# Attention on one core: the V product of a unit is copied out of PSUM in two halves, by ScalarE and by VectorE

## The chip, the cores and the metric

The kernel runs on one core of a Trainium2 chip. The core has a matrix engine (TensorE, PE in the profile, its weight loads PEld), three engines for elementwise work (VectorE or DVE, ScalarE or ACT, GpSimd or POOL) and SyncE (SP), which here only issues DMA transfers. Each engine works through its own queue in order, and they wait for each other by semaphores. TensorE writes its products to PSUM, eight banks of 128 partitions by 512 fp32 columns; the other engines bring them from there to SBUF. The metric is the device time of one execution in microseconds. A change of the kernel counts as a change of time from 0.2% on.

## The reference

One transformer block on 2048 tokens of width 512, with adaptive layer norms. Attention has 32 heads of width 16, softmax over all 2048 keys, and a feed-forward part of width 1792 follows.

```
h = layernorm(x) * (1 + ca) + sa                  # sa, ca, ga, ... = silu(c) @ w_mod
q, k, v = split_heads(h @ wqkv)                   # 32 heads of 16
p = softmax(q @ k.T / 4)
x = x + ga * ((p @ v) merged @ wo)
h = layernorm(x) * (1 + cb) + sb
x = x + gb * (gelu(h @ w1 + b1) @ w2 + b2)
```

## The kernel before

The program has three stages. In the first, up to about 304 us, it normalizes the tokens, transposes them and computes Q, K and V; it also begins with the row maxima of the scores. The second is attention, up to about 1411 us. The third is the output projection and the feed-forward part.

**Units and steps.** Attention runs over 32 units. A unit u is a group of 4 heads and a block of 512 queries (`g, qb = divmod(u, NB)`). A unit has 16 steps of 128 keys, numbered through as s (`NS = NU * NKC` of them). In a step TensorE makes four score blocks of 128 keys by 512 queries, one for each head (`exp_step`, L860, tokens X0 to X3, tile sc), ScalarE takes the exponential of each (L861, tile p), and TensorE multiplies the four blocks of the step before with V (`pv_step`, L693, token P). The four heads of a V product go to four column groups of the array, so that one PSUM tile pv holds 32 rows for each head: 16 rows of the product, then the row of the denominators. The sum over the unit's 16 steps is formed in that tile.

**Row maxima.** The exponentials of a unit need its row maxima. They are made ahead: a step also has three maxima blocks (tokens M0 and M1, `max_bank`): a matmul into a tile mx (L429) and a row maximum of its 512 columns on VectorE (L431). When a unit's 64 are done, a small reduction (L465), two GpSimd instructions and a transpose (L475) bring them into the form in which they are stored and loaded as additional rows of Q. For the first nine units this happens in the first stage, so the maxima run out some 20 steps before the end of attention.

**Order.** The order within a step is written out by hand and alternates between two lists; the V product P of step s - 1 stands in step s:

```
ORDER = ("X0 X1 M1 X2 M0 X3 P M1".split(), "X0 X1 X2 M0 M0 X3 P M1".split())
```

After a step's tokens come the other tasks that are due there: `todo` (among them the transpose of L475) and `hooks` (among them the split of the output weights, with a cast on VectorE, L709, at steps 24, 32, 40 and 48). PSUM in this stage has 3 banks for mx, 4 for sc and 1 for pv. So the last V product of a unit, the copy of its tile and the first V product of the next unit follow one another on one bank.

**The copy.** When the last step's V product has been issued, in step s = 16(u + 1), `attn_out` copies pv into the SBUF tile osb (128 by 512, two buffers) by one ScalarE activation (L680) and issues five stores: the products of the four heads (L682) and the denominators (L683). They are read again, as o and den, only when the output projection of that query block is near.

Of the kernel before, what the change touches and what calls it, by code (L numbers as in the profile page):

```python
# [10 lines left out]
AF = mybir.ActivationFunctionType  # L11
# [14 lines left out]
TB = S // NB  # L26
# [26 lines left out]
def block_kernel(ctx: ExitStack, tc: tile.TileContext, x, wqkv, wo, w1, b1, w2, b2, c, w_mod, out):  # L53
    nc = tc.nc
    te, ve, ac, gp, sy = nc.tensor, nc.vector, nc.scalar, nc.gpsimd, nc.sync
# [621 lines left out]
    def attn_out(u, pv):  # L677
        g, qb = divmod(u, NB)
        o = ppool.tile([P, TB], F32, tag="osb", name="osb")
        ac.activation(o, pv, AF.Copy)  # L680
        for j in range(4):
            sy.dma_start(o_d[qb][g * 64 + j * DH : g * 64 + (j + 1) * DH], o[32 * j : 32 * j + DH])  # L682
        sy.dma_start(den_d[qb][g * 4 : (g + 1) * 4], o[DH::32])  # L683
# [3 lines left out]
    def pv_step(s):  # L687
        u, kc = divmod(s, NKC)
        g = u // NB
        if kc == 0:  # L690
            cur_pv[0] = bank_pv()
        for j in range(4):
            te.matmul(cur_pv[0][32 * j : 32 * (j + 1)], vg[g][:, kc, j * VW : j * VW + 32],  # L693
                      pt.pop((s, j)), start=kc == 0, stop=kc == NKC - 1)
        if kc == NKC - 1:
            attn_out(u, cur_pv[0])
# [329 lines left out]
```

## Time and profile before

| | |
|---|---|
| time, median of 3 runs (lowest to highest) | 1770.09 us (1769.41 to 1771.3) |
| the profiled execution | 1768.67 us |
| its span, from the first to the last instruction | 1766.9 us |
| mean granted TensorE clock | 0.995 |
| ScalarE, exponentials of L861 | 2048 instructions, 1055.3 us busy, mean 615 ns |
| VectorE, row maxima of L431 | 1472 instructions, 927.9 us busy, mean 684 ns |
| ScalarE, the copies of L680 | 32 instructions, 20.3 us busy, mean 633 ns |

A row of a timeline has the start in us from the start of the span, the length in us, the engine, the line of the kernel, the operation, output and input tile, shapes and the number of instructions merged in it; in square brackets the idle time of that engine before it and what ended that. A row of a group or of one line has the number of instructions and the least, median and largest duration in ns. A busy time can hold instructions that overlap in their engine's pipeline: the next one may start before the end of the last.

### The profile page before, as it was taken

How to read it: one execution, taken by the hardware profiler on the slowest of the kernel's cores; microseconds unless marked ns; L12 is line 12 of the kernel's file. 1: busy time of each engine (PE TensorE's matmuls, PEld its weight loads, DVE VectorE, ACT ScalarE, POOL GpSimd, SP SyncE). 2: the span in 40 equal slices, each digit the busy share in tenths (PEclk: the TensorE clock that was granted, in tenths of full speed). 3: DMA queues.
4: the chain of work that ended last, by engine and by line, in shares of the span. 5: the costliest groups of instructions: out<-in, count | busy, mean ns of one | idle time of the engine just before them, and what ended most of it. 6: DMA issues, size and time to landing. Idle time of an engine off the chain costs nothing.

```text
span 1766.9 us, 29171 instructions
## 1 busy us (share of the span) xinstructions
PE 1750.8 (99%) x10554; PEld 902.6 (51%) x10554; DVE 1405.3 (80%) x2553; ACT 1356.4 (77%) x2580; POOL 320.1 (18%) x347
## 2 busy tenths in 40 slices
PE   8999999999999999999999999999999999999998
PEld 6755555343343343343343334334333478788887
DVE  6579998898888888888888888888886286838453
ACT  3478887999999999999999999999999722213222
POOL 3204422011000000000000000000003154636462
PEclk9999999999999999999999999999999999999999
DMA  8767636811500410410411101101013064323341
GB/s 278 252 137 163 150 115 132 128 36 29 86 23 23 77 32 23 74 35 23 74 30 28 39 23 35 38 23 35 23 58 106 21 195 131 126 78 113 103 120 48
DMA packets 124100, 144.17 MB, mean 82 GB/s; under 512 B 38930, under 2 KB 72722, under 8 KB 122004
## 3 DMA queue, kind: packets, MB, share of 16 engines
q1 hardware_dynamic: 120644, 135.55, 30.6%
q10 hardware_dynamic: 3312, 6.76, 1.0%
q8 instruction: 83, 1.36, 0.3%
q14 instruction: 61, 0.50, 0.1%
HBM read 106.37 MB, written 35.87 MB: 81 GB/s over the span
## 4 chain that ended last, share of the span: by engine, by line
PE 93%; DVE 3%; issue 1%; DMA 1%; POOL 1%; SPq 0%; ACT 0%; ACTq 0%; DVEq 0%; POOLq 0%
PE pv L693 29%; PE mx L429 19%; PE sc L300 16%; PE sc L860 13%; PE mx L447 6%; PE mx L924 5%; PE pv L924 2%; PE sc L800 1%; PE mx L800 1%; DVE glo L907 0%; POOL w2l L731 0%; PE sc L257 0%; DMA rb<-rden 0%; PE mx L257 0%; DVE xin L278 0%
## 5 line engine op out<-in xcount | busy, mean ns | idle before, releaser
L861 ACT ACTIVATE p<-sc 128x512 f32<-128x512 f32 x2048 | 1055.3, 615 | 42.3 <-PE sc L860 16.8
L431 DVE TENSOR_REDUCE mxs<-mx 128x1 f32<-128x512 f32 x1472 | 927.9, 684 | 116.0 <-PE sc L860 78.6
L693 PE MATMUL pv<-p,vg 128*32 128x512 f32 x4096 | 546.8, 605 | 0.0
L860 PE MATMUL sc<-qst,kq 50*128 50x512 f32 x1024 | 284.7, 437 | 1.6 <-DVE mxf L458 1.6
L860 PE MATMUL sc<-qst,kt 50*128 50x512 f32 x1024 | 282.3, 431 | 0.0
L429 PE MATMUL mx<-kq,qmx 48*128 48x512 f32 x768 | 262.2, 428 | 0.2
L429 PE MATMUL mx<-kt,qmx 48*128 48x512 f32 x704 | 241.5, 430 | 0.0
L429 PEld LDWEIGHTS mx<-kq,qmx 48*128 48x128 f32 x768 | 122.6, 184 | 228.4 <-DVE mxs L431 209.3
L429 PEld LDWEIGHTS mx<-kt,qmx 48*128 48x128 f32 x704 | 114.0, 186 | 209.1 <-DVE mxs L431 191.5
L903 ACT ACTIVATE g<-sc,b_c 128x512 f32<-128x512 f32 x56 | 38.6, 690 | 237.2 <-PE sc L300 237.2
L458 DVE CUSTOM_DVE_ANT_0 cp<-mx,cp 128x512 f32<-128x512 f32 x288 | 186.9, 688 | 36.3 <-PE mx L447 31.4
L471 POOL CAST m<-mn 128x16 fp32r<-128x16 f32 x32 | 6.3, 197 | 1029.4 <-DVE mn L465 1029.4
L454 ACT ACTIVATE cp<-mx 128x512 f32<-128x512 f32 x288 | 156.4, 597 | 38.4 <-PE mx L447 38.1
L693 PEld LDWEIGHTS pv<-p,vg 128*32 128x32 f32 x4096 | 81.1, 108 | 181.2 <-issue 169.8
L860 PEld LDWEIGHTS sc<-qst,kq 50*128 50x128 f32 x1024 | 126.4, 186 | 33.7 <-ACT p L861 23.4
L907 DVE TENSOR_TENSOR glo<-g,ghi 128x512 fp32r<-128x512 f32 x56 | 60.2, 1075 | 94.7 <-ACT ghi L906 94.7
L860 PEld LDWEIGHTS sc<-qst,kt 50*128 50x128 f32 x1024 | 125.6, 185 | 10.1 <-ACT p L861 3.1
L447 PE MATMUL mx<-kt,qmx 48*128 48x512 f32 x576 | 113.0, 455 | 0.0
L729 POOL TENSOR_TENSOR w1l<-w1r,w1h 128x512 fp32r<-128x512 f32 x56 | 76.9, 1372 | 152.7 <-DVE w1h L728 130.5
L447 PEld LDWEIGHTS mx<-kt,qmx 48*128 48x128 f32 x576 | 58.3, 184 | 56.0 <-issue 33.8
L300 PE MATMUL sc<-hThi,w 128*128 128x512 f32 x256 | 84.1, 436 | 2.2 <-DVE hThi L263 2.2
L731 POOL TENSOR_TENSOR w2l<-w2r,w2h 128x512 fp32r<-128x512 f32 x56 | 81.1, 1448 | 6.6 <-DVE w2h L730 6.1
(158 smaller groups left out, 1672.8 us busy)
## 6 DMA issues: line engine op xcount, KB each, us to landing
w1r<-in_B_w_dram SPq DMA_DIRECT2D x56, 256.0 KB
w2r<-in_B_w_dram SPq DMA_DIRECT2D x56, 256.0 KB
qk<-parts SPq DMA_DIRECT2D x25, 512.0 KB
qmx<-qk SPq DMA_DIRECT2D x192, 64.0 KB
qst<-qk SPq DMA_DIRECT2D x192, 64.0 KB
wmod<-in_w_mod_dram SPq DMA_DIRECT2D x6, 1024.0 KB
kq<-qk SPq DMA_DIRECT2D x24, 256.0 KB
kt<-qk SPq DMA_DIRECT2D x24, 256.0 KB
```

Source lines behind the costliest of these rows:

```text
L300: te.matmul(ps, p, q, start=i == 0, stop=i == len(terms) - 1)
L429: te.matmul(ps, qmx[u][rows, p, qc * P : (qc + 1) * P], kst[u // NB][rows, p, kr * TB : (kr + 1) * TB], start=True, stop=True)
L431: ve.tensor_reduce(mxs[u][:, p, a, qc, kr : kr + 1], ps, axis=AX.X, op=ALU.max, negate=True)
L447: te.matmul(ps, qmx[u][rows, p, qc * P : (qc + 1) * P], kpm[u // NB][rows, p, t0 : t0 + TB], start=True, stop=True)
L454: ac.activation(vabs[n, a], ps, AF.Abs)
L458: ve.tensor_tensor_reduce(v, ps, v, -0.5, 3.0e38, ALU.add, ALU.min, mxs[u][:, p, a, qc, r : r + 1])
L693: te.matmul(cur_pv[0][32 * j : 32 * (j + 1)], vg[g][:, kc, j * VW : j * VW + 32], pt.pop((s, j)), start=kc == 0, stop=kc == NKC - 1)
L729: gp.tensor_tensor(alo, a, ahi.bitcast(F32), op=ALU.subtract)
L731: gp.tensor_tensor(blo, b, bhi.bitcast(F32), op=ALU.subtract)
L860: te.matmul(ps, k[r0 : r0 + KX, p, kc * P : (kc + 1) * P], q[r0 : r0 + KX, p], start=True, stop=True)
L861: ac.activation(pb, ps, AF.Exp, scale=SCALE)
L924: te.matmul(acc[qb][t], p[:, sl], q, start=f == 0 and n == 0, stop=f == NF - 1 and n == 2)
```

## The change

The one copy of 128 partitions by 512 columns becomes two of 256 columns. The first half of the queries is copied by ScalarE as before, the second half by VectorE with a plain copy. Source, destination, the five stores and the order of everything else stay the same; in VectorE's queue the new instruction stands where `attn_out` is called. In the changed kernel the lines behind it have numbers larger by 2.

```diff
     def attn_out(u, pv):
         g, qb = divmod(u, NB)
         o = ppool.tile([P, TB], F32, tag="osb", name="osb")
-        ac.activation(o, pv, AF.Copy)
+        h = TB // 2
+        ac.activation(o[:, :h], pv[:, :h], AF.Copy)
+        ve.tensor_copy(o[:, h:], pv[:, h:])
         for j in range(4):
             sy.dma_start(o_d[qb][g * 64 + j * DH : g * 64 + (j + 1) * DH], o[32 * j : 32 * j + DH])
         sy.dma_start(den_d[qb][g * 4 : (g + 1) * 4], o[DH::32])
```

## Prediction

> **What bounds the kernel now.** I read the page's busy shares first, then the busy time by stage, the waits of the attention stage, and last the timeline of one unit boundary, engine by engine.
>
> ```profile
> span 1766.9 us, 29171 instructions
> PE 1750.8 (99%) x10554; PEld 902.6 (51%) x10554; DVE 1405.3 (80%) x2553; ACT 1356.4 (77%) x2580; POOL 320.1 (18%) x347
> ...
> PE 93%; DVE 3%; issue 1%; DMA 1%; POOL 1%; SPq 0%; ACT 0%; ACTq 0%; DVEq 0%; POOLq 0%
> ...
> 304.00:1411.00 1107.00, 1106.80 (x7661) 440.75 (x7659) 947.18 (x1547) 1065.03 (x2079) 48.61 (x82) 1.00 0.21 45
> ```
>
> The chain that ends last is TensorE. In the attention stage (the last row: length, then the busy time of PE, PEld, DVE, ACT and POOL) ScalarE is busy for 1065 of 1107 us and VectorE for 947, so neither has much room. A busy PE may still be waiting inside its stream, so the pace must be read from something that recurs: the V product of each 128-key step. Its weight loads near one boundary, and near the first and the last of the 30 boundaries that look like this:
>
> ```profile
> 341.96 0.16 PEld L693 LDWEIGHTS pv<-p,vg 128*32 128x32 f32 x8 [0.36 <-ACT osb L680]
> 344.29 0.16 PEld L693 LDWEIGHTS pv<-p,vg 128*32 128x32 f32 x8 [0.25 <-issue]
> ...
> 645.59 0.16 PEld L693 LDWEIGHTS pv<-p,vg 128*32 128x32 f32 x8 [0.36 <-issue]
> 647.72 0.16 PEld L693 LDWEIGHTS pv<-p,vg 128*32 128x32 f32 x8 [0.37 <-issue]
> 649.83 0.16 PEld L693 LDWEIGHTS pv<-p,vg 128*32 128x32 f32 x8 [0.36 <-ACT osb L680]
> 652.15 0.16 PEld L693 LDWEIGHTS pv<-p,vg 128*32 128x32 f32 x8 [0.25 <-issue]
> ...
> 1333.48 0.16 PEld L693 LDWEIGHTS pv<-p,vg 128*32 128x32 f32 x8 [0.37 <-ACT osb L680]
> 1335.78 0.16 PEld L693 LDWEIGHTS pv<-p,vg 128*32 128x32 f32 x8 [0.24 <-issue]
> ```
>
> A step takes 2.12 us (645.59 to 647.72, 647.72 to 649.83). One step per unit takes 2.32 (649.83 to 652.15; 2.33 at the first, 2.30 at the last): 0.20 us lost, one step after the copy. The product at 649.83 is named as waiting for the copy, but its 0.36 us of load idleness is what 645.59 and 647.72 have too, so the copy's release costs nothing there. What costs is the next row:
>
> ```profile
> 648.60 0.62 ACT L861 ACTIVATE p<-sc 128x512 f32<-128x512 f32 x1
> 649.08 0.63 ACT L680 ACTIVATE osb<-pv 128x512 f32<-128x512 f32 x1
> 650.51 0.67 ACT L861 ACTIVATE p<-sc 128x512 f32<-128x512 f32 x1
> ...
> 651.23 0.18 PEld L860 LDWEIGHTS sc<-qst,kt 50*128 50x128 f32 x1
> ...
> 651.72 0.18 PEld L860 LDWEIGHTS sc<-qst,kt 50*128 50x128 f32 x1 [0.20 <-ACT p L861]
> ```
>
> ScalarE's ends lie 0.49 us apart when it has a queue (648.60 + 0.62 = 649.22, 649.08 + 0.63 = 649.71). Four exponentials per step are 1.96 of 2.12 us, so the copy, a fifth, puts it behind, the score banks come free late (651.18, and the load at 651.23), and TensorE stands 0.20 us. Over the boundaries the copy costs 30 x 0.20 = 6.1 us now. That is all that can be won.
>
> **What the change removes.** Half of the copy's columns leave ScalarE. No row shows a 256-column activation, so I take the price from both ends:
>
> ```profile
> L191 ACT ACTIVATE s_c<-c_c x1: 205/205/205, 2.9 to 2.9; 128x4 f32<-128x4 f32 x1
> ...
> L680 ACT ACTIVATE osb<-pv x32: 597/633/686, 341.2 to 1410.9; 128x512 f32<-128x512 f32 x32
> ```
>
> From 4 to 512 columns 597 - 205 = 392 ns, 0.77 ns a column, so 256 fewer save 0.20 us: ScalarE's slot goes from 0.49 to 0.30 us. Bounds: 0.245 (no fixed part) and 0.49 (nothing saved). With 0.30 its backlog falls from 0.49 - 0.16 = 0.33 to 0.14 us, and the 0.20 us stand behind the score banks all but disappears, if nothing else is late.
>
> **What it adds, and where.** The instruction order of the changed program puts VectorE's half behind the two row maxima of that step and ahead of the third. It shows three waits that the diff does not: VectorE's copy waits for ScalarE (not for TensorE), the first V product of the next unit waits for VectorE, and so does the store. So the halves do not run side by side; they form a chain of ScalarE, VectorE, TensorE, and what is queued on VectorE behind the copy waits with it: the row maxima, which free the three mx banks that TensorE's maxima matmuls need.
>
> The Trainium skill speaks for that wait: "PSUM — Partial Sum Buffer", section "PSUM bank collisions raise a hardware error", says that two engines may not touch one bank and 32-partition group at once, reads of disjoint columns included, and that only semaphores keep them apart. Both halves lie in one bank; no run here shows a collision. By the rule the gain of halves run side by side is not to be had.
>
> VectorE's rows and the two handoffs:
>
> ```profile
> 647.73 0.68 DVE L431 TENSOR_REDUCE mxs<-mx 128x1 f32<-128x512 f32 x1
> 648.33 0.68 DVE L431 TENSOR_REDUCE mxs<-mx 128x1 f32<-128x512 f32 x1
> 649.25 0.69 DVE L431 TENSOR_REDUCE mxs<-mx 128x1 f32<-128x512 f32 x1 [0.24 <-PE sc L860]
> 649.86 0.68 DVE L431 TENSOR_REDUCE mxs<-mx 128x1 f32<-128x512 f32 x1
> 650.45 0.68 DVE L431 TENSOR_REDUCE mxs<-mx 128x1 f32<-128x512 f32 x1
> ...
> L223 DVE COPY modc<-sc x2: 150/150/151, 17.4 to 50.7; 128x4 f32<-128x4 f32 x2
> ...
> L709 DVE CAST wo_hi<-wo_raw x4: 416/417/418, 359.1 to 410.2; 128x512 fp32r<-128x512 f32 x4
> ...
> 1603.11 0.63 ACT L906 ACTIVATE ghi<-g 128x512 fp32r<-128x512 f32 x1
> ...
> 1603.77 1.70 DVE L907 TENSOR_TENSOR glo<-g,ghi 128x512 fp32r<-128x512 f32 x1 [1.25 <-ACT ghi L906]
> ```
>
> The copy's price: out of PSUM a 4-column copy takes 0.15 us, a 512-column row maximum 0.68; halfway, 0.41 us. Bounds: a 512-column cast out of SBUF takes 0.417, so at that pace 0.15 + (0.417 - 0.15)/2 = 0.28; and 0.68 if half the columns saved nothing. I take 0.41, since the maximum is the row that reads PSUM. The next VectorE instruction starts some 0.08 us before the end of the last (0.68 long, 0.60 apart), so the copy holds the queue for 0.33 us.
>
> The Trainium skill weighs in on the pace: "VectorE: DVE Perf Modes", section "Why PSUM operands drop a tier", caps a copy of fp32 out of PSUM at the plain rate, where another table of the page has row maxima too. The sum by the rule is the one at 0.41 us, by the cast's row the one at 0.28.
>
> Now the boundary at 649, step by step:
> - ScalarE's half ends at 649.22 + 0.30 = 649.52; VectorE starts 0.03 us later (1603.11 + 0.63 to 1603.77), at 649.55. VectorE was free from 648.93 on and stands that long.
> - The copy ends at 649.96. A product waiting for VectorE loads about 0.05 us after (651.18 to 651.23 for ScalarE; the same for VectorE below): 650.02 in place of 649.83. **First loss, 0.19 us.**
> - The row maximum that ran at 649.25 starts at 649.55 + 0.33 = 649.88, the next two at 650.48 and 651.08; the last ends at 651.76, and its bank's matmul weights load at 651.81.
>
> What such lateness costs can be read elsewhere, where a cast pushed the maxima back by as much as 0.33 us:
>
> ```profile
> 359.12 0.16 PEld L693 LDWEIGHTS pv<-p,vg 128*32 128x32 f32 x8 [0.36 <-issue]
> ...
> 360.81 0.18 PEld L429 LDWEIGHTS mx<-kt,qmx 48*128 48x128 f32 x1 [0.16 <-DVE mxs L431]
> ...
> 361.23 0.16 PEld L693 LDWEIGHTS pv<-p,vg 128*32 128x32 f32 x8 [0.24 <-issue]
> ```
>
> The product came 0.43 us after the late load and 2.11 after the one before: no loss, but no room left either, since with the maxima of a step side by side it comes no sooner after the last of them. Here the product comes at 651.81 + 0.43 = 652.24, and without this wait at 650.02 + 2.12 = 652.14. **Second loss, 0.10 us.** In the step after, VectorE has caught up: three maxima are 3 x 0.60 = 1.80 of 2.12 us.
>
> So 0.29 us are lost at a boundary that lost 0.20. The two losses together are the time of ScalarE's slot plus VectorE's 0.33, less 0.34 that stay hidden.
>
> At some boundaries something else follows on VectorE. By the instruction order a transpose comes directly after the first delayed maximum at 7 of them, and the cast of L709 at 2:
>
> ```profile
> 581.43 0.20 DVE L475 STREAM_TRANSPOSE mt<-m 128x32 f32<-128x32 f32 x1
> 581.56 2.08 DVE L431 TENSOR_REDUCE mxs<-mx 128x1 f32<-128x512 f32 x3
> ```
>
> They add 0.13 and 0.33 us, now without cover: 7 x 0.13 + 2 x 0.33 = 1.6 us. At the 31st boundary no maxima are left, and I put the exchange of ScalarE time for a later release at zero; the copy of the last unit runs while TensorE is in the output projection and its bank is next used 20 us later, so also zero. The five stores per unit move by under 0.3 us on a queue that TensorE doesn't wait for.
>
> Sum: 30 x 0.29 + 1.6 - 6.1 = +4.2 us; a first maximum after idleness holds VectorE for 0.61 us (649.25 to 649.86), not 0.60, 30 x 0.01 more: +4.5. The profiled execution took 1768.67 us, so 1773.2; the median of the runs shown is 1770.09, 1.4 above it, and the forecast for a median is **1774.6 us**.
>
> **The rivals.**
> 1. *VectorE's copy is fast* (not slower). At 0.28 us it holds the queue for 0.20; the loss is 0.13 less, 0.16 a boundary: 30 x 0.16 + 1.6 - 6.1 = +0.3, so 1770.4. For it: the cast's 0.417. Against it: that reads SBUF. It breaks even at a copy of 0.27 us and is within 0.2% of before from 0.38 downwards.
> 2. *The change does what it says*: the halves overlap, the copy ends before 649.7 and the maxima are hardly late; the 6.1 us go, 1764.0. Against it: the wait for ScalarE in the order. It decides if the copy's start in the trace lies before ScalarE's end.
> 3. *Dearer halves*: a fixed part that leaves ScalarE near 0.45 or VectorE near 0.6 us adds 0.15 to 0.2 a boundary: 1779 to 1780.5. Against it: both slopes above. At both upper bounds (0.49 and 0.68) the loss is 0.19 + 0.27 more, 30 x 0.46 = 14 us: 1788.
>
> **How the numbers follow.** Forecast 0.70, rival 1 0.16, rival 2 0.06, rival 3 0.08. The forecast's own spread, from 0.02 to 0.03 us on each of two halves times 30, is 1772.5 to 1777. The range goes down to rival 1 and a little up into rival 3: 1770.2 to 1778. No change, for this kernel within 0.2% (3.5 us: 1766.6 to 1773.6), holds rival 1 and the lower edge of the forecast, 0.24; slower 0.69; faster, rival 2 and a little of rival 1's, 0.07.
>
> **What would show it.** VectorE's copies of about 0.41 us starting 0.03 after ScalarE's halves of about 0.44; the first V product of a unit idle for VectorE's copy, its step 2.3 us; the next step 2.2, released by a row maximum and no longer by an exponential; ScalarE's waits behind the score banks gone. Wrong would be: copies that start beside ScalarE's, a step after the boundary of 2.12, or boundaries that still wait for exponentials.

## Result and profile after

| | before | after |
|---|---|---|
| time, median (lowest to highest), 13 runs each | 1770.47 us (1768.67 to 1774.03) | 1775.41 us (1772.72 to 1778.07) |
| ratio to before, 95% interval | | 1.0021 (1.0011 to 1.0030) |
| span of the profiled execution | 1766.9 us | 1771.9 us |

Slower, and clear of no change, but only just by the 0.2% from which a change counts here: the interval reaches down to 1.0011. The ratio of 1.0021 stands for 3.7 us, the medians lie 4.9 apart.

From the page of the changed kernel: span, busy shares, and the chain by engine.

```profile
span 1771.9 us, 29277 instructions
PE 1751.5 (99%) x10554; PEld 898.9 (51%) x10554; DVE 1412.4 (80%) x2585; ACT 1352.1 (76%) x2580; POOL 320.0 (18%) x347
...
PE 88%; DVE 4%; ACT 4%; issue 2%; DMA 1%; POOL 1%; SPq 1%; ACTq 0%; DVEq 0%; POOLq 0%
```

TensorE's busy time is the same. ScalarE has lost 4 us of work and VectorE has gained 7, yet less of the chain is TensorE's (88% in place of 93%) and more is ScalarE's (4% in place of 0) and VectorE's (4% in place of 3%).

The boundary shown of before, in the changed kernel: the weight loads (PEld) first, then ScalarE and VectorE.

```profile
648.87 0.16 PEld L695 LDWEIGHTS pv<-p,vg 128*32 128x32 f32 x8 [0.36 <-issue]
651.00 0.16 PEld L695 LDWEIGHTS pv<-p,vg 128*32 128x32 f32 x8 [0.37 <-issue]
653.29 0.16 PEld L695 LDWEIGHTS pv<-p,vg 128*32 128x32 f32 x8 [0.54 <-DVE osb L682]
655.08 0.18 PEld L429 LDWEIGHTS mx<-kq,qmx 48*128 48x128 f32 x1 [0.27 <-DVE mxs L431]
655.51 0.16 PEld L695 LDWEIGHTS pv<-p,vg 128*32 128x32 f32 x8 [0.24 <-issue]
...
651.88 0.62 ACT L863 ACTIVATE p<-sc 128x512 f32<-128x512 f32 x1
652.36 0.42 ACT L681 ACTIVATE osb<-pv 128x256 f32<-128x256 f32 x1
...
652.81 0.42 DVE L682 COPY osb<-pv 128x256 f32<-128x256 f32 x1 [0.52 <-ACT osb L681]
653.15 3.07 DVE L431 TENSOR_REDUCE mxs<-mx 128x1 f32<-128x512 f32 x5
```

VectorE stands idle for 0.52 us until ScalarE's half has ended (652.36 + 0.42 = 652.78), copies from 652.81 on, and only then takes up the maxima. The first product of the new unit comes 2.29 us after the last (653.29 - 651.00), released by VectorE's copy. The next comes after 2.22, 0.43 us behind a maxima load that waited for a row maximum. At a boundary with a transpose, and at one with a cast, that second step is longer:

```profile
584.66 0.16 PEld L695 LDWEIGHTS pv<-p,vg 128*32 128x32 f32 x8 [0.51 <-DVE osb L682]
586.98 0.16 PEld L695 LDWEIGHTS pv<-p,vg 128*32 128x32 f32 x8 [0.25 <-issue]
...
378.19 0.16 PEld L695 LDWEIGHTS pv<-p,vg 128*32 128x32 f32 x8 [0.54 <-DVE osb L682]
380.74 0.16 PEld L695 LDWEIGHTS pv<-p,vg 128*32 128x32 f32 x8 [0.24 <-issue]
```

2.32 and 2.55 us. Read off all 30 boundaries in this way, the two steps take 2.30 and 2.27 us on average, 0.32 us lost; before, 2.12 and 2.32, 0.20 lost. 30 times the difference is 3.6 us, the size of the ratio.

The groups of the two halves (number, least, median and largest duration in ns):

```profile
L681 ACT ACTIVATE osb<-pv x32: 384/418/473, 343.0 to 1416.0; 128x256 f32<-128x256 f32 x32
...
L682 DVE COPY osb<-pv x32: 424/424/426, 343.5 to 1416.4; 128x256 f32<-128x256 f32 x32
```

### The profile page after: what moved, and what is told of

It reads as the page before. It is cut to its first block, busy times and chain, and to the rows that moved or that the text cites. A ratio compares the mean times of both kernels' runs of the same rounds, so it can differ in the third digit from the quotient of the medians.

```text
span 1771.9 us, 29277 instructions
## 1 busy us (share of the span) xinstructions
PE 1751.5 (99%) x10554; PEld 898.9 (51%) x10554; DVE 1412.4 (80%) x2585; ACT 1352.1 (76%) x2580; POOL 320.0 (18%) x347
## 4 chain that ended last, share of the span: by engine, by line
PE 88%; DVE 4%; ACT 4%; issue 2%; DMA 1%; POOL 1%; SPq 1%; ACTq 0%; DVEq 0%; POOLq 0%
PE pv L695 27%; PE mx L429 19%; PE sc L300 16%; PE sc L862 11%; PE mx L447 6%; PE mx L926 5%; ACT p L863 3%; PE pv L926 2%; PE sc L802 1%; DVE osb L682 1%; PE mx L802 1%; DVE mxs L431 1%; ACT osb L681 1%; DVE glo L909 0%; POOL w2l L733 0%
```

## Experiments

All ratios are to the kernel before, run beside each. "First" and "second" are the steps after a boundary; 2.12 us is a step without loss.

### Which wait costs: no shared bank

```diff
-        o = ppool.tile([P, TB], F32, tag="osb", name="osb")
-        ac.activation(o[:, :h], pv[:, :h], AF.Copy)
-        ve.tensor_copy(o[:, h:], pv[:, h:])
+        oa = ppool.tile([P, h], F32, tag="osa", name="osa")
+        ob = ppool.tile([P, h], F32, tag="osb", name="osb")
+        ac.activation(oa, pv[:, :h], AF.Copy)
+        ve.tensor_tensor(ob, ga_b[:, :h], gb_b[:, :h], op=ALU.add)
...
```

Each half is stored by five DMAs of its own; those lines are left out here. The second half of each V product is never copied.

> ScalarE copies its half into a tile of its own; VectorE fills the other half's tile from two SBUF tiles with an addition of about the same length as its copy, so the second half of each V product is left out, and neither engine waits for the other. Twice as many stores, half as long. Theory: VectorE works as long as in the change but waits for nothing, so the maxima are on time and the product waits for ScalarE's half alone, early: loss 0.00 to 0.02 us a boundary, 1764 (6 us faster than before). Rival (VectorE's work costs, not its wait): the second of the two losses, 0.10 us a boundary and 0.10 to 0.34 more at nine of them, stays: 1767 to 1769.

Ratio 0.9962 (0.9946 to 0.9978). The product's loads near 651 and the group of VectorE's addition:

```profile
649.33 0.16 PEld L697 LDWEIGHTS pv<-p,vg 128*32 128x32 f32 x8 [0.37 <-issue]
651.44 0.16 PEld L697 LDWEIGHTS pv<-p,vg 128*32 128x32 f32 x8 [0.36 <-ACT osa L682]
653.56 0.16 PEld L697 LDWEIGHTS pv<-p,vg 128*32 128x32 f32 x8 [0.26 <-issue]
```

```profile
L683 DVE TENSOR_TENSOR osb<-ga_b,gb_b x32: 415/416/1105, 344.7 to 1406.1; 128x256 f32<-128x256 f32 x32
```

2.11 and 2.12 us: no loss. VectorE works as long (0.42 us) at the same place of its queue; only the waits are gone, VectorE's for ScalarE and that of the next unit's product for VectorE. So 0.42 us of VectorE's time are free here, the chain of waits is what costs, and ScalarE's half is short enough for the exponentials. (Under "Without a chain" below the product does wait for VectorE, but VectorE not for ScalarE, and a plain boundary loses nothing either.) One of the 30 boundaries did lose time: near 1331 the addition took 1.10 us, the largest duration of its group, and the second step 2.46. Why it was long there is not known.

### What makes the wait: a tile for each half

The same two tiles and ten stores, with `ve.tensor_copy(ob, pv[:, h:])` as in the change.

> The change with a tile of its own for each half, stored by ten shorter stores; both halves still read the one PSUM bank. Theory: the wait of VectorE for ScalarE is there for the PSUM bank alone, so the losses are the change's: 2.30 and 2.22 at a plain boundary, time as the change, 1774 to 1776. Rival (it is the shared output tile that ties the halves together): they overlap, loss near 0, 1764.

Ratio 1.0034 (1.0019 to 1.0049).

```profile
652.78 0.16 PEld L697 LDWEIGHTS pv<-p,vg 128*32 128x32 f32 x8 [0.37 <-issue]
655.08 0.16 PEld L697 LDWEIGHTS pv<-p,vg 128*32 128x32 f32 x8 [0.54 <-DVE osb L683]
657.30 0.16 PEld L697 LDWEIGHTS pv<-p,vg 128*32 128x32 f32 x8 [0.24 <-issue]
```

2.30 and 2.22 again. The PSUM tile that both halves read, one bank, is enough for the wait. The shared output tile alone may be enough as well; that was not run by itself. The median, 1777.2 us, lies above the expected 1774 to 1776, though the boundaries are those of the change; five of these seven runs had a mean granted clock of 0.992 or 0.993, against 5 of the 26 runs of the kernel before beside them.

### The other order

```diff
-        ac.activation(o[:, :h], pv[:, :h], AF.Copy)
         ve.tensor_copy(o[:, h:], pv[:, h:])
+        ac.activation(o[:, :h], pv[:, :h], AF.Copy)
```

> The two halves in the other order: VectorE copies first, ScalarE waits for it. Theory: VectorE's copy runs where it is free anyway (maxima 0.01 us late), the product of the next unit is released about 0.02 us late, but ScalarE stands idle some 0.3 us before a half of 0.30, so its exponentials end 0.09 us later than with its full copy: the second step loses 0.29 us, released by an exponential again, at every boundary, with nothing more at transposes and casts: 30 x 0.29 - 6.1 = 2.6 us slower than before (1772 to 1773). Rival (the lateness of the maxima is all that the change costs): loss 0, 1764.

Ratio 1.0013 (1.0002 to 1.0024).

```profile
652.24 0.16 PEld L695 LDWEIGHTS pv<-p,vg 128*32 128x32 f32 x8 [0.37 <-issue]
654.35 0.16 PEld L695 LDWEIGHTS pv<-p,vg 128*32 128x32 f32 x8 [0.36 <-ACT osb L682]
656.72 0.16 PEld L695 LDWEIGHTS pv<-p,vg 128*32 128x32 f32 x8 [0.24 <-issue]
```

```profile
PEld sc L862 <- ACT p L863: 5.5, 28, 0.2
```

2.11 and 2.37, the second again released by exponentials, as before the change (the last row is from the waits of its weight loads: total in us, number, longest; it is the row that the kernel before has too). The first loss of the change is gone and the second is 0.25 us in place of the expected 0.29. Not expected were the 7 boundaries with a transpose, which take 2.35 and 2.38: there a unit's small reduction (L465) stands ahead of the copy in VectorE's queue, the copy starts later, and ScalarE waits longer.

### The second loss alone: a maximum moved

```diff
+        if 0 < u < NU - 1 and kc == 2:
+            toks = "X0 X1 M1 X2 X3 P M1".split()
+        if 0 < u < NU - 1 and kc == 4:
+            toks = "X0 X1 M1 X2 M0 M0 X3 P M1".split()
```

> The change, with the first-half maximum of the second step after a boundary moved two steps later, behind the one there. Theory: the second loss comes from that maximum's matmul, which waits for a bank; without it the second step is 2.12 again, the first stays at 2.30 (it waits for VectorE's copy): loss 0.18 a boundary, so about 0.15 x 30 = 4 us less than the change, 1770 to 1771. Rival (the second step is late because of the exponentials, or follows from the first): the second step stays at 2.22, time as the change, 1774 to 1775.

Ratio 1.0099 (1.0076 to 1.0122), 18 us slower, where about the time of before was expected.

```profile
654.74 0.16 PEld L695 LDWEIGHTS pv<-p,vg 128*32 128x32 f32 x8 [0.37 <-issue]
657.03 0.16 PEld L695 LDWEIGHTS pv<-p,vg 128*32 128x32 f32 x8 [0.54 <-DVE osb L682]
659.15 0.16 PEld L695 LDWEIGHTS pv<-p,vg 128*32 128x32 f32 x8 [0.36 <-issue]
661.26 0.16 PEld L695 LDWEIGHTS pv<-p,vg 128*32 128x32 f32 x8 [0.36 <-issue]
...
663.54 0.18 PEld L429 LDWEIGHTS mx<-kq,qmx 48*128 48x128 f32 x1 [0.73 <-DVE mxs L431]
...
663.97 0.16 PEld L695 LDWEIGHTS pv<-p,vg 128*32 128x32 f32 x8 [0.25 <-issue]
```

The steps: 2.29, 2.12, 2.11, 2.71. The first keeps its loss and the second has none, as expected, so the second loss does come with that maximum; in the change its matmul's load is the one at 655.08, which waited for a row maximum. But four maxima in one step don't fit: the load of the last one's matmul waits 0.73 us for a row maximum (663.54), the product comes 0.43 us after it, and that step takes 0.59 us more at each of the 30 boundaries (17.7 us). The total was mispredicted for a cost that the experiment brought in itself.

### The work behind the copy, moved away

In the change, the casts two steps later (`s0 = 22 + 8 * k`), and the small reduction and what follows it two steps later where a unit's maxima end in the last step of another unit:

```diff
-    def next_max(a):
+    def next_max(a, late=False):
...
-        return [] if left[u] else [max_rows(u)]
+        if left[u]:
+            return []
+        return [lambda: todo.append(lambda: todo.append(max_rows(u)))] if late else [max_rows(u)]
...
-                new += next_max(int(tok[1]))
-        for f in todo[:1]:
-            f()
-        todo = todo[1:] + new
+                new += next_max(int(tok[1]), kc == NKC - 1)
+        if todo:
+            todo.pop(0)()
+        todo += new
```

> The change, with the casts and the small reductions and transposes moved away from the boundaries. Theory: they add 0.10 us at 7 boundaries and 0.34 at 2, behind the delayed maxima, 1.4 us in all, and nothing elsewhere; the plain boundary's 0.28 stays: 1.4 us less than the change, 2.2 us slower than before (1772 to 1773). Rival (they cost the same wherever they stand): time as the change, 1774 to 1776.

Ratio 1.0022 (1.0008 to 1.0036): the times can't tell 1.4 us. The steps can. A boundary that had a transpose:

```profile
581.96 0.16 PEld L697 LDWEIGHTS pv<-p,vg 128*32 128x32 f32 x8 [0.36 <-issue]
584.26 0.16 PEld L697 LDWEIGHTS pv<-p,vg 128*32 128x32 f32 x8 [0.55 <-DVE osb L684]
586.48 0.16 PEld L697 LDWEIGHTS pv<-p,vg 128*32 128x32 f32 x8 [0.24 <-issue]
```

2.30 and 2.22, as at a plain one, and so at all 30 (on average 2.30 and 2.22). The casts and transposes cost only behind the delayed maxima.

### The two lengths in a row: halves by rows

```diff
-        h = TB // 2
-        ac.activation(o[:, :h], pv[:, :h], AF.Copy)
-        ve.tensor_copy(o[:, h:], pv[:, h:])
+        h = P // 2
+        ac.activation(o[:h], pv[:h], AF.Copy)
+        ve.tensor_copy(o[h:], pv[h:])
```

> The copy split by partitions: 64 rows with all 512 columns by ScalarE, the other 64 by VectorE; the built order has VectorE wait for ScalarE as in the change. Theory: an operation's time goes by columns, so each half takes the time of a whole copy (0.49 us of ScalarE's slot, 0.60 of VectorE's queue), and by the formula of the prediction a boundary loses 0.49 + 0.60 - 0.34 = 0.75 us: about 0.65 in the first step, 0.1 in the second; 30 x 0.75 + 1.4 - 6.1 = 18 us slower than before (1788). Rival (the loss is the handoff between the engines, not the two lengths in a row): as the change, 1775.

Ratio 1.0117 (1.0098 to 1.0136), 21 us slower. VectorE and the product's loads:

```profile
658.63 0.69 DVE L682 COPY osb<-pv 64x512 f32<-64x512 f32 x1 [0.70 <-ACT osb L681]
659.36 3.68 DVE L431 TENSOR_REDUCE mxs<-mx 128x1 f32<-128x512 f32 x6
...
656.64 0.16 PEld L695 LDWEIGHTS pv<-p,vg 128*32 128x32 f32 x8 [0.37 <-issue]
659.38 0.16 PEld L695 LDWEIGHTS pv<-p,vg 128*32 128x32 f32 x8 [0.99 <-DVE osb L682]
661.72 0.16 PEld L695 LDWEIGHTS pv<-p,vg 128*32 128x32 f32 x8 [0.24 <-issue]
```

A plain boundary takes 2.74 and 2.34 us, 0.84 lost, and 0.90 on average over the 30. The copy of 64 rows is as long as one of 128, and it holds the queue for 0.73 us, not for the 0.60 expected; with that the formula gives 0.49 + 0.73 - 0.34 = 0.88. The two halves share no row of their tiles here, and VectorE waits for ScalarE all the same (0.70 us).

### Without a chain: the whole copy on VectorE

```diff
-        h = TB // 2
-        ac.activation(o[:, :h], pv[:, :h], AF.Copy)
-        ve.tensor_copy(o[:, h:], pv[:, h:])
+        ve.tensor_copy(o, pv)
```

> The whole copy by VectorE, none of it by ScalarE. Theory (the chain of waits ScalarE, VectorE, TensorE is what costs): the copy needs no ScalarE, starts about 0.32 us earlier against the second row maximum than the change's copy does (0.03 us after nothing but the end of that maximum), takes 0.69 us and ends before the next unit's product is due; the maxima are 0.27 us late, which is within the 0.33 us that cost nothing; ScalarE loses its fifth operation. Loss 0 in the two steps after a plain boundary, 0.07 where a transpose follows, 0.27 where a cast follows: 1.0 us in all in place of 6.1, so 5 us faster than before (1765). Rival (VectorE's time in front of the maxima is what costs): the queue is held 0.60 us in place of 0.33, so 0.27 us a boundary more than the change loses, 8 us slower than the change (1783).

Ratio 0.9979 (0.9968 to 0.9991). VectorE at the boundary near 650, the product's loads there, and those of a boundary with a transpose:

```profile
649.91 0.68 DVE L680 COPY osb<-pv 128x512 f32<-128x512 f32 x1
650.50 3.12 DVE L431 TENSOR_REDUCE mxs<-mx 128x1 f32<-128x512 f32 x5
...
648.70 0.16 PEld L693 LDWEIGHTS pv<-p,vg 128*32 128x32 f32 x8 [0.37 <-issue]
650.81 0.16 PEld L693 LDWEIGHTS pv<-p,vg 128*32 128x32 f32 x8 [0.36 <-DVE osb L680]
652.92 0.16 PEld L693 LDWEIGHTS pv<-p,vg 128*32 128x32 f32 x8 [0.29 <-issue]
...
580.43 0.16 PEld L693 LDWEIGHTS pv<-p,vg 128*32 128x32 f32 x8 [0.37 <-issue]
582.62 0.16 PEld L693 LDWEIGHTS pv<-p,vg 128*32 128x32 f32 x8 [0.41 <-DVE osb L680]
584.95 0.16 PEld L693 LDWEIGHTS pv<-p,vg 128*32 128x32 f32 x8 [0.25 <-issue]
```

Twice the work on VectorE, and a plain boundary loses nothing (2.11 and 2.11): with no ScalarE in the chain, the copy follows the maximum without a pause. The transposes' boundaries lose 0.28 (2.19 and 2.33), not 0.07: the small reduction ahead of the copy was left out of that expectation. The casts' lose 0.27, as expected.

Once more, beside the next kernel's repetition and the change's:

> The whole copy by VectorE, once more. Theory: 0.28 us lost at 7 boundaries and 0.27 at 2, none at the rest: 3.6 to 4.4 us below before, a ratio of 0.9975 to 0.9980. Rival (no boundary matters): as the one beside it.

Ratio 0.9979 (0.9968 to 0.9990).

### A kernel without a boundary loss

The whole copy on VectorE, with the casts and the small reductions moved as above.

> The whole copy by VectorE, and VectorE's other small work kept away from the boundaries: the four casts of the output weights two steps later, and a unit's small reduction, GpSimd steps and transpose two steps later where they fall on the boundary (7 units). Theory: the 7 and 2 boundaries that still lost time with the whole copy on VectorE (0.28 and 0.27 us: 2.5 us in all) have the small reduction ahead of the copy and the transpose or cast behind it in VectorE's queue; without them every boundary takes 2.12 and 2.12, loss 0, so 6 us faster than before (1764) and 2.5 us faster than the whole copy on VectorE alone. Rival (VectorE's 0.60 us a boundary costs by itself somewhere): stays at 1766 to 1767.

Ratio 0.9975 (0.9962 to 0.9987). The boundary that had a transpose:

```profile
580.27 0.16 PEld L695 LDWEIGHTS pv<-p,vg 128*32 128x32 f32 x8 [0.36 <-issue]
582.40 0.16 PEld L695 LDWEIGHTS pv<-p,vg 128*32 128x32 f32 x8 [0.37 <-DVE osb L682]
584.53 0.16 PEld L695 LDWEIGHTS pv<-p,vg 128*32 128x32 f32 x8 [0.32 <-issue]
```

Both steps 2.13, and 2.12 and 2.12 over all 30: nothing is lost at any. The first timing didn't separate this kernel from the one before it, so both ran again, with the change:

> The whole copy by VectorE with its other small work moved away, once more beside the next two on one chip. Theory (no boundary loses time): 6.0 to 6.6 us below before, a ratio of 0.9963 to 0.9966, and 2 us below the whole copy on VectorE alone. Rival (the steps of the profile don't carry over to the time): no difference from the whole copy alone.

Ratio 0.9952 (0.9937 to 0.9968), median 1763.19 us against 1771.73 before; its interval touches but does not overlap the one of the whole copy alone. It beats both the kernel before and the changed one. The 8.5 us are more than the 6 that the boundaries account for, and the first timing showed 4.4; four of these five runs had a mean granted clock of 0.995 or 0.996, against 7 of the 23 runs of the kernel before beside them, so part of the rest may be the clock.

> The change, once more. Theory: its boundaries lose 0.32 us on average in place of 0.20: 3.3 to 3.6 us above before, a ratio of 1.0019 to 1.0021. Rival (part of the first comparison's 4.9 us between the medians is in the change, outside the boundaries): a ratio of 1.0028.

Ratio 1.0015 (1.0002 to 1.0027). The steps at the boundaries are those of the first profile (2.30 and 2.27 on average). The interval takes in the 1.0019 to 1.0021 of the boundaries and leaves out 1.0028, if only by 0.0001, while that of the first comparison takes it in. So nothing asks for a cost outside the boundaries, but one of about 1 us isn't ruled out. This ratio alone lies below 0.2%.

## Why the prediction was right

The forecast was 1774.6 us, 4.5 above before; the ratio gives 3.7, the boundaries 3.6.

- *What bounds.* That the 0.20 us before came from exponentials, not from the copy's release, held: without a wait and with a short half on ScalarE (no shared bank) the loss went at 29 of the 30 boundaries, and with the whole copy off ScalarE the plain boundaries lost nothing. In the changed kernel no weight load of a score waits for an exponential at the boundaries any more, where before 28 did (the row shown at the other order).
- *Prices.* ScalarE's half ends at 652.78, 0.28 us after the exponential before it (651.88 + 0.62); forecast 0.30. The copy takes 0.424, forecast 0.41, and holds the queue for 0.34 (652.81 to 653.15), forecast 0.33. It does not run at the pace of the cast out of SBUF, so rival 1 falls. The Trainium skill, "VectorE: DVE Perf Modes", section "Why PSUM operands drop a tier", has the plain rate for such a copy. The traces agree: 256 columns took 0.424 us and 512 (the whole copy on VectorE) 0.68, as long as a row maximum of 512.
- *The chain.* VectorE's copy starts 0.03 us after the end of ScalarE's half (652.78 to 652.81), as forecast. That this costs is shown by taking the sharing of the bank away (no loss) and by keeping it with separate output tiles (the same loss). Rival 2, halves side by side, falls.
- *First loss*, forecast 0.19: 0.18. *Second loss*, forecast 0.10: 0.10, and it goes when that maximum is moved.
- *Work behind the copy*: 0.33 at a cast (2.55 against 2.22), forecast 0.33; 0.10 at a transpose, forecast 0.13; both gone when it is moved.
- *Size.* The sum has 30 x 0.30 + 1.6 = 10.6 us lost, the boundaries show 30 x 0.32 = 9.6. The surplus is in several terms, each by 0.01 to 0.03 us a boundary: ScalarE's slot, the first loss, the transposes, and the 0.01 for a maximum after idleness, which isn't there (five maxima in 3.07 us, so 0.60 apart). That the median, 1775.41, lies so near 1774.6 is in part luck: by the ratio and by the boundaries the sum is 0.8 to 0.9 us too high. The 31st boundary, put at zero, took 6.37 us for its three steps before and 6.35 after. Rival 3 would have needed halves far above 0.42 us.

What the prediction did not look for is which work stands *ahead* of the copy in VectorE's queue. It made no difference to the change, whose copy waits longer for ScalarE anyway (the first step is 2.30 at the transposes too), and it was the miss in two later expectations.

## What to carry to other kernels

Halving an operation over two engines paid here only where the halves did not wait for each other. When both read one PSUM bank, the program may put them in a row, as it did here, and the second engine's queue then stands behind the first engine. Look for the waits in the built order, price what is queued behind the waiting instruction, and see what stands ahead of it. If an engine with a little slack can do the whole operation at a moment when it is free, that can be cheaper than half of it: here all of the copy on VectorE costs nothing at a plain boundary, and half of it 0.28 us.

## What else the runs showed

The copy of partitions 64 to 127 holds VectorE's queue longer than a copy or a maximum of 128 partitions: 0.73 against 0.59 (649.91 to 650.50 in the whole copy on VectorE) at the same length of 0.69 and 0.68 us. The next instruction starts 0.04 us after its end and not 0.09 before it. Why was not tried.

Executions of one kernel differ by 2 us and more, outside the steps of attention. The two profiles of the whole copy on VectorE, 1765.6 and 1764.0 us long, are 1.73 us apart at the first boundary already (341.69 and 339.96) and 1.58 at the last (1366.24 and 1364.66). Part of such differences goes with the granted clock: beside the experiment with two tiles the kernel before took 1769.6 us on average in its 12 runs with a mean clock of 0.995, and 1774.7 in the 5 with 0.992 or 0.993. Each row has the stretch, its length, the busy times, then the clock's share of full speed; the first two are before, the third is the whole copy on VectorE:

```profile
304.00:310.00 6.00, 6.00 (x24) 2.82 (x21) 3.85 (x7) 4.10 (x9) 1.30 (x2) 0.51 0.70 156
...
1520.00:1536.00 16.00, 13.74 (x60) 10.78 (x59) 14.27 (x16) 3.88 (x6) 11.86 (x9) 1.00 0.60 202
```

```profile
1520.00:1536.00 16.00, 13.75 (x54) 10.87 (x53) 14.78 (x17) 2.64 (x4) 11.44 (x9) 0.89 0.70 226
```

For some us the clock is about half, at places that differ between executions: 0.51 from 304 to 310 before, 0.50 from 306 to 310 in the changed kernel, and in the whole copy on VectorE 0.51 from 1528 to 1530, where the kernel before keeps 1.00. So differences of 1 or 2 us between kernels were read from the steps at the boundaries, where the clock was 1.00 (from 320 to 1410, in every profile), and not from a time.
